# Sliding-window attention and a gated convolution block in one kernel: queries of each head in four runs of 144, one copy of x, nine buffers for layer one

## Chip, cores and metric

One core of a Trainium2 chip runs the whole problem in one program. The metric is the device time of an execution in microseconds, the median of three runs.

## The reference

```python
def _attn_ref(q, k, v):                      # 8 batches, 8 heads, 576 positions, 64 wide
    scores = scale * np.matmul(q, k.transpose(0, 1, 3, 2))
    rel = pos[:, None] - pos[None, :]
    mask_plain = (rel >= 0) & (rel < 32)                         # heads 0 to 3
    mask_dil = (rel >= 0) & (rel < 128) & (rel % 4 == 0)         # heads 4 to 7
    attn = softmax(np.where(mask, scores, -1e9))
    return np.matmul(attn, v)

def _moe_ref(x, w_in, conv_w, w_out):        # x: 576 x 512, w_in: 512 x 1024, w_out: 1024 x 512
    h = np.maximum(x @ w_in, 0.0)
    conv_out = conv_w[0] * h[t-1] + conv_w[1] * h[t] + conv_w[2] * h[t+1]
    gate = 1.0 / (1.0 + np.exp(-conv_out))
    return h * gate @ w_out
```

The attention of the eight heads, laid side by side, is x. All inputs are float32, except that the weights reach the kernel as float64.

## The kernel before, in words

The work of a batch is four attention units and one expert. A unit (`attention(b, p)`) is a pair of heads: p = 0, 1 are plain pairs (kind 0), p = 2, 3 dilated ones (kind 1). Each head's 576 queries are cut into 18 blocks of 32; a block sees 64 keys. For kind 1 the positions are first sorted by their remainder modulo 4, which makes four runs of 144 positions, and the two heads of a pair lie on partitions 0 to 63 and 64 to 127 of the tile `qk`.

A unit runs in these steps. **Scores** (L258): one float32 matmul for each block and head, 64 rows by 32 columns of the array, 64 moving columns; each is carried out as two passes. The 32 blocks 0 to 15 of the two heads go round eight places of the array (two row halves by four column quadrants). Blocks 16 and 17 go to slot 8, each head to two quadrants of its own; for kind 1 each of them is two accumulating matmuls, because it joins two runs. So kind 0 has 36 matmuls (72 passes) and kind 1 has 40 (80 passes). **Softmax**: VectorE adds the mask while it takes the scores out of PSUM (L270), then maximum, exponential, sum, reciprocal, product and a 32x32 transpose into `pt`; in the eight units of batches 0 and 1 ("slotwise") the exponential is nine small ScalarE instructions (L279). **Values** (L306): 48 float32 matmuls (96 passes), 32 rows by 64 columns. In both kinds head 0 of turn t reads row quadrant t and head 1 row quadrant t+2, so that eight matmuls in a row use eight places. The sixteen queries at the end of each run are the tail: for kind 0, eight matmuls of 32 columns, for kind 1 sixteen of 16 columns, and both go round four places only. **x**: ScalarE copies the result out of PSUM in two pieces (512 and 64 columns, L344) as the rounded part x a; the rest x b is made on VectorE in two pieces (L361), or, in the eight units of batches 0 and 1 ("helped"), by TensorE subtracting x a (L351, L354) and ScalarE copying twice (L359).

The expert of a batch: **layer one** (L386) is 192 matmuls of 128x128 by 288 columns into PSUM buffers `mm` (`mm` and `nn` for batch 0), which ScalarE takes out as `h` (L393, three buffers of `h`); the **gating** of each of eight `h` is a scaled copy and a sigmoid on ScalarE (L404, L409), two convolution taps, a product and a subtraction on VectorE (L398, L411, L415) and a copy on ScalarE (L413); **layer two** (L431) is 96 or 120 matmuls of 512 columns (batch 0: 192 of 256 columns), copied out (L441) and stored. Eight chunks of weights are converted from float64 by VectorE and ScalarE (L495 to L510), four for each layer.

Scores, values and the helped subtraction share one PSUM buffer, `att` (four banks), so only one unit at a time can be between its scores and their mask, or between its values and x. `qk` has two buffers, `v`, `s` three, `pt` two, `x` seven.

The order is not written by hand. Every step is a `Task` with an engine, a cost and a due time from the table `DUE`; `Planner.order` runs through them once while the kernel is built: of the tasks that could start within 0.25 of the earliest one, the smallest due time goes first. All engines and the SyncE queue then run their instructions in this fixed order.

Of the kernel before, what the change touches and what calls it, by code (L numbers as in the profile page):

```python
# [34 lines left out]
F32 = mybir.dt.float32  # L35
F32R = mybir.dt.float32r
BF16 = mybir.dt.bfloat16
# [10 lines left out]
W = 64  # L48
# [3 lines left out]
RES, RL = 4, S // 4  # L52
QD = 512 + 96
GW = S + 64
PAIRED = 1024
KP, KD = S + 32, S + 4 * 32 + 16
# [3 lines left out]
    "first": (72.60, 66.90, 228.40, 589.20, 119.60, 531.50, -87.70, 234.00),  # L60
    "gated": (82.90, 155.90, 204.60, -64.70, 127.90, -15.10, -48.50, 110.30),
    "second": (-142.00, 377.30, 377.60, 656.90, 397.40, 693.20, 129.60, 375.60),
    "weights": (22.30, 130.00, 960.40, -10.60, 117.40, 161.20, -241.40, 43.40),
    "fetch": (-112.90, -48.10, -47.30, -45.60, -28.50, 201.40, 419.40, 547.40),
    "conv": -231.90,
    "scores": ((-40.40, 79.70, 181.60, 63.80), (575.40, -0.50, -254.50, -6.60), (-12.70, 246.70, 160.70, 78.10), (268.20, 239.00, 217.70, 56.80), (487.10, 188.70, 220.00, 145.40), (395.00, 150.90, 159.50, -40.20), (543.40, 173.10, 228.00, 68.60), (-21.90, 798.30, 440.60, 187.40)),
    "softmax": ((12.30, -11.50, -273.80, 13.00), (22.20, -301.50, 79.30, 22.70), (-286.10, -37.40, 501.50, 612.80), (635.70, 444.80, 605.40, -27.20), (153.60, 396.90, 188.40, 295.10), (656.80, 106.40, -81.80, -42.50), (235.70, -1.40, -85.60, 184.20), (232.80, 6.50, 691.70, 114.60)),
    "values": ((-76.40, -82.10, -0.30, 335.00), (-211.50, 25.20, 1.90, -28.10), (116.70, -15.80, -40.30, -53.90), (-11.40, 77.90, 236.90, -27.60), (-87.20, -68.40, 562.90, 200.90), (59.40, -256.40, 258.50, -9.80), (-14.50, -9.70, 112.40, 606.40), (45.10, -17.50, 111.30, 181.20)),
    "queries": ((-58.30, -253.50, -98.80, -122.30), (-54.90, -11.80, -3.80, -15.00), (110.30, 156.80, 72.10, 148.70), (8.70, 82.80, 166.20, 190.90), (186.60, 202.10, 242.60, 251.80), (233.50, 430.00, 377.50, 300.80), (394.10, 432.30, 301.90, 701.90), (873.40, 615.20, 466.90, 684.00)),
    "runs": ((19.00, 45.50, -38.60, -73.00), (115.60, 104.90, 122.90, -52.00), (115.50, 92.60, 155.60, 124.30), (164.20, 194.60, 225.50, 235.00), (285.30, 234.30, 338.60, 404.50), (368.80, 827.50, 555.70, 555.10), (848.60, 650.80, 306.50, 543.70), (874.70, 433.60, 855.90, 838.60)),  # L70
# [102 lines left out]
def attn_moe(ctx: ExitStack, tc: tile.TileContext, qk_p, qk_d, v_p, v_d, w_in, w_out, conv, mask, out):  # L173
# [19 lines left out]
    slots("qk", 2, [128, QD + KD])  # L193
# [7 lines left out]
    hs = slots("h", 3, [128, S + 2])  # L201
# [22 lines left out]
    def queries(p, qk, hd, n):  # L224

        qk = qk[hd * 64:hd * 64 + 64]
        if p < 2:
            return [(qk[:, n * 32:n * 32 + 32], qk[:, S + n * 32:S + n * 32 + W])]
        key = lambda r, i: qk[:, QD + r * (RL + 32) + i * 32:QD + r * (RL + 32) + i * 32 + W]
        if n < 16:  # L230
            return [(qk[:, n * 32:n * 32 + 32], key(n // 4, n % 4))]
        g = n - 16
        q0 = 512 + g * 48
        return [(qk[:, q0 + 16 * i:q0 + 16 * i + 32], key(2 * g + i, 4)) for i in range(2)]
# [3 lines left out]
    def attention(b, p):  # L238
# [5 lines left out]
        n = (S + KP, QD + KD)[kind]  # L244
# [3 lines left out]
            out=v.t, in_=(v_p, v_d)[kind][b, p % 2]), uses=[v])  # L248

        def scores():  # L250


            for n in [4 * t + i for i in range(4) for t in range(4)] + [16, 17]:
                for hd in range(2):
                    slot, quad = place(hd, n)
                    parts = queries(p, qk.t, hd, n)
                    for i, (q, k) in enumerate(parts):
                        nc.tensor.matmul(sc.t[quad * 32:quad * 32 + 32, slot // 4, slot % 4 * W:slot % 4 * W + W], q, k,  # L258
                                         start=i == 0, stop=i == len(parts) - 1, skip_group_check=True)

        last = plan.add("PE", (0.8, 0.92)[kind], due, scores, [lq], [qk, sc, s], "S")
# [12 lines left out]
        if slotwise:  # L274
# [7 lines left out]
            last = plan.add("ACT", 2.7, soft + 1.5, exps, [last], [s, m, z], "exp")  # L282
# [15 lines left out]
        def values():  # L298
# [18 lines left out]
            for kh in range(2):  # L317
                for r in range(1 + kind):
                    for g, hd in turns[:4]:
                        c0 = 512 + 32 * kh  # L320
                        if kind == 0:
                            pv(2 * hd + g, hd, g, 10 + kh, c0, 128, 32)
                        else:
                            pv(2 * hd + g, hd, g, 8 + 2 * kh + r, c0 + 16 * r, 128 + 16 * r, 16)

        last = plan.add("PE", (0.9, 0.85)[kind], val + 0.0, values, [lv, last], [v, pt, tv, x], "V")

        def parts(t):

            main, rest = t[:, 0:512], t[:, 512:S]  # L330
            if kind == 0:
                return main.rearrange("c (q m) -> c q m", q=4), rest.rearrange("c (g m) -> c g m", g=2)
            return main.rearrange("c (m r) -> c m r", r=RES), rest.rearrange("c (m g r) -> c m g r", g=2, r=2)

        def src(i):
            main, rest = tv.t[:, :, 0:128], tv.t[:, 0:2, 128:160]
            if kind == 0:
                return (main, rest)[i]
            return (main.rearrange("c r m -> c m r"), rest.rearrange("c g (r m) -> c m g r", r=2))[i]

        pieces = (0, 0.62), (1, 0.25)
        his = []
        for i, cost in pieces[::-1]:
            last = plan.add("ACT", cost, val + 1.0, lambda i=i: nc.scalar.copy(out=parts(x.t[0])[i], in_=src(i)),  # L344
                            [last, *his], [tv, x])
            his.append(last)
# [275 lines left out]
```

## Time and profile before

| | |
|---|---|
| median of 3 runs | 536.16 us (535.06 to 536.45) |
| the profiled execution | 535.56 us, its span 533.8 us |
| TensorE matmul busy | 505.9 us, 95% of the span |
| VectorE busy | 397.3 us, 74% |
| ScalarE busy | 303.7 us, 57% |
| bytes moved | 52.24 MB, 98 GB/s on average |

The span runs from the first to the last instruction; the time lies 1.8 us above it. Matmul time is counted from an instruction's start to its end, and since matmuls are pipelined, starts and their distances tell more than busy time.

### The profile page before, as it was taken

How to read it: one execution, taken by the hardware profiler on the slowest of the kernel's cores; microseconds unless marked ns; L12 is line 12 of the kernel's file. 1: busy time of each engine (PE TensorE's matmuls, PEld its weight loads, DVE VectorE, ACT ScalarE, POOL GpSimd, SP SyncE). 2: the span in 40 equal slices, each digit the busy share in tenths (PEclk: the TensorE clock that was granted, in tenths of full speed). 3: DMA queues.
4: the chain of work that ended last, by engine and by line, in shares of the span. 5: the costliest groups of instructions: out<-in, count | busy, mean ns of one | idle time of the engine just before them, and what ended most of it. 6: DMA issues, size and time to landing. Idle time of an engine off the chain costs nothing.

```text
span 533.8 us, 17819 instructions
## 1 busy us (share of the span) xinstructions
PE 505.9 (95%) x8048; PEld 449.4 (84%) x8048; DVE 397.3 (74%) x611; ACT 303.7 (57%) x660; POOL 1.0 (0%) x15
## 2 busy tenths in 40 slices
PE   3569999999999999999999999999999999999996
PEld 2459899998877998789977899789988899789985
DVE  5987999998986799859996569828997277607900
ACT  4975998638632587237742377517764386427710
POOL 0000000000000000000000000000000000000000
PEclk9999999999999999999999999999999999999999
DMA  8846721233145312451224401321313100110011
GB/s 301 297 164 210 241 60 31 80 127 101 43 170 163 97 32 79 154 182 59 83 67 149 148 33 48 121 96 53 104 47 119 52 2 1 59 42 1 0 50 50
DMA packets 16556, 52.24 MB, mean 98 GB/s; under 512 B 2016, under 2 KB 3168, under 8 KB 15456
## 3 DMA queue, kind: packets, MB, share of 16 engines
q1 hardware_dynamic: 16336, 51.02, 28.6%
q8 instruction: 63, 1.03, 0.8%
q14 instruction: 13, 0.11, 0.1%
q10 hardware_dynamic: 144, 0.08, 0.1%
HBM read 41.66 MB, written 9.44 MB: 96 GB/s over the span
## 4 chain that ended last, share of the span: by engine, by line
PE 80%; DVE 8%; ACT 7%; DMA 3%; issue 1%; ACTq 0%
PE nn L431 34%; PE mm L386 31%; PE att L306 8%; PE att L258 4%; ACT s L279 3%; PE nn L386 2%; DVE c L398 2%; PE att L351 1%; DMA qk<-in_qk_p_dram 1%; DVE t L501 1%; DVE wo L510 1%; ACT c L409 1%; DMA c<-in_mask_dram 1%; DVE c L411 1%; DVE g L415 1%
## 5 line engine op out<-in xcount | busy, mean ns | idle before, releaser
L431 PE MATMUL nn<-wo,g 128*128 128x512 f32 (+1 forms) x960 | 212.0, 375 | 0.0
L431 PEld LDWEIGHTS nn<-wo,g 128*128 128x128 f32 x960 | 163.4, 188 | 33.4
L398 DVE SCALAR_TENSOR_TENSOR c<-h,conv_sb,c 128x576 f32<-128x576 f32 x128 | 103.5, 816 | 32.8 <-ACT c L404 31.1
L393 ACT ACTIVATE h<-mm 128x288 f32<-128x288 f32 x120 | 48.5, 408 | 43.9 <-PE mm L386 40.8
L441 ACT COPY out<-nn 128x512 f32<-128x512 f32 (+1 forms) x40 | 21.7, 542 | 72.5 <-PE nn L431 45.1
L413 ACT CAST g<-c 128x576 fp32r<-128x576 f32 x64 | 42.4, 672 | 17.7 <-DVE c L411 15.7
L411 DVE TENSOR_TENSOR c<-c,h 128x576 f32<-128x576 f32 x64 | 47.9, 756 | 5.9 <-ACT c L409 5.4
L306 PEld LDWEIGHTS att<-pt,v 32*64 32x64 f32 x3072 | 41.2, 140 | 13.1 <-issue 8.5
L415 DVE TENSOR_TENSOR g<-c,g 128x576 fp32r<-128x576 f32 x64 | 47.6, 755 | 4.5 <-ACT g L413 3.4
L404 ACT ACTIVATE c<-h,conv_sb 128x576 f32<-128x576 f32 x64 | 49.4, 778 | 1.3
L386 PE MATMUL mm<-x1a,wi 128*128 128x288 f32 x176 | 49.7, 297 | 0.0
L258 PE MATMUL att<-qk 64*32 64x64 f32 x2432 | 36.6, 237 | 13.4 <-DMA qk<-in_qk_p_dram 5.3
L258 PEld LDWEIGHTS att<-qk 64*32 64x32 f32 x2432 | 30.4, 112 | 22.2 <-issue 7.7
L409 ACT ACTIVATE c<-c 128x576 f32<-128x576 f32 x64 | 43.2, 684 | 10.3 <-DVE c L398 9.4
L306 PE MATMUL att<-pt,v 32*64 32x64 f32 (+2 forms) x3072 | 44.7, 234 | 3.8 <-DVE s L270 1.3
L386 PE MATMUL mm<-x2a,wi 128*128 128x288 f32 x144 | 41.6, 304 | 1.3 <-ACT h L393 1.3
L386 PE MATMUL mm<-x0a,wi 128*128 128x288 f32 x144 | 40.6, 297 | 0.0
L270 DVE TENSOR_TENSOR s<-att,mask_sb 128x512 f32<-128x512 f32 x64 | 26.6, 450 | 16.3 <-PE att L258 16.2
L386 PE MATMUL mm<-x6a,wi 128*128 128x288 f32 x128 | 36.6, 301 | 0.8 <-ACT h L393 0.7
L386 PE MATMUL mm<-x5a,wi 128*128 128x288 f32 x128 | 36.2, 298 | 0.2 <-ACT h L393 0.2
L386 PE MATMUL mm<-x4a,wi 128*128 128x288 f32 x128 | 35.9, 295 | 0.0
L295 DVE STREAM_TRANSPOSE pt<-s 128x576 f32<-128x576 f32 x32 | 24.8, 776 | 11.9 <-PE att L306 10.9
(134 smaller groups left out, 808.7 us busy)
## 6 DMA issues: line engine op xcount, KB each, us to landing
qk<-in_qk_d_dram SPq DMA_DIRECT2D x16, 664.0 KB, 4.3
qk<-in_qk_p_dram SPq DMA_DIRECT2D x16, 592.0 KB, 4.1
out_dram<-out SPq DMA_DIRECT2D x28, 256.0 KB, 2.2
v<-in_v_d_dram SPq DMA_DIRECT2D x16, 384.0 KB, 3.1
v<-in_v_p_dram SPq DMA_DIRECT2D x16, 384.0 KB, 3.4
raw<-in_w_in_dram SPq DMA_DIRECT2D x4, 1024.0 KB, 6.6
raw<-in_w_out_dram SPq DMA_DIRECT2D x4, 1024.0 KB, 4.7
out_dram<-out SPq DMA_DIRECT2D x16, 128.0 KB, 2.4
```

The costliest lines, as they stand in the source:

```text
L258: nc.tensor.matmul(sc.t[quad * 32:quad * 32 + 32, slot // 4, slot % 4 * W:slot % 4 * W + W], q, k, start=i == 0, stop=i == len(parts) - 1, ...
L270: last = plan.add("DVE", cost, soft + 0.0, lambda i=i: nc.vector.tensor_tensor(out=two(flat())[i], in0=scored()[i], in1=two(masked)[i], op ...
L306: nc.tensor.matmul(tv.t[hd * 64:hd * 64 + 64, bank, o:o + n], v.t[quad * 32:quad * 32 + 32, block // 2, block % 2 * 64:block % 2 * 64 + 64 ...
L386: nc.tensor.matmul(ps.t[:, 0:HALF], wi[jw][fc // 2][:, fc % 2, k], x[k].t[jx][:, hf * HALF:hf * HALF + HALF], start=(k == 0 and i == 0), s ...
L393: relu.append(plan.add("ACT", 0.4, due + 1.6 * u + 1.6, lambda fc=fc, hf=hf, ps=ps: nc.scalar.activation(out=h[fc].t[:, 1 + hf * HALF:1 + ...
L398: nc.vector.scalar_tensor_tensor(out=c[fc].t, in0=h[fc].t[:, k:S + k], scalar=conv_sb[:, k, fc:fc + 1], in1=c[fc].t, op0=ALU.mult, op1=ALU ...
L404: t = plan.add("ACT", 0.777, d, lambda fc=fc: nc.scalar.activation(out=c[fc].t, in_=h[fc].t[:, 1:S + 1], func=AF.Copy, scale=conv_sb[:, 1, ...
L409: t = plan.add("ACT", 0.686, d + 1.0, lambda fc=fc: nc.scalar.activation(out=c[fc].t, in_=c[fc].t, func=AF.Sigmoid), [t], [c[fc]], "sigmoid")
L411: t = plan.add("DVE", 0.755, d + 1.5, lambda fc=fc: nc.vector.tensor_tensor(out=c[fc].t, in0=c[fc].t, in1=h[fc].t[:, 1:S + 1], op=ALU.mult ...
L413: hi = plan.add("ACT", 0.675, d + 2.0, lambda fc=fc: nc.scalar.copy(out=half(fc, 0), in_=c[fc].t), [t, *(done[fc] if odd else [])], [c[fc] ...
L415: lo = plan.add("DVE", 0.755, d + 2.5, lambda fc=fc: nc.vector.tensor_tensor(out=half(fc, 1), in0=c[fc].t, in1=half(fc, 0).bitcast(F32), o ...
L431: nc.tensor.matmul(ps.t[:, 0:n], g[k // 2].t[:, k % 2, jg, c0:c0 + 128], w.rearrange("p h c -> p (h c)") if hf is None else w[:, hf], star ...
```

## The change

In both kinds a head's queries are now four runs of 144; run t goes to quadrant t, for both heads. The last 16 queries of run t of both heads share the 32 rows of quadrant t in slot 8: the queries are laid out with zeros under the other head, and one score matmul over all 128 rows makes both heads' scores. These four matmuls come first. Scores thus have 36 matmuls in both kinds. In values both heads of turn t read row quadrant t; the tail has sixteen matmuls of 16 columns in both kinds, going round eight places; two matmuls of kind 0 over padding alone are left out. x is copied in one piece of 576 columns, and the helped subtraction is four matmuls of 144 columns in place of four of 128 and two of 32. `h` has nine buffers. The `DUE` table is replaced whole, so the order of nearly all work moves; some planner costs change. The `qk` transfers grow from 592 and 664 KB to 632 and 680 KB, those of `v` of kind 1 shrink from 384 to 320 KB. One argument of the program's builder makes room for the added buffers.

```diff
-QD = 512 + 96
+RUN = S // 4
+QW = 512 + 128
+STEP = RUN, RUN + 32
+KEYS = S + 48, S + 4 * 32 + 16
...
-    "gated": (82.90, 155.90, 204.60, -64.70, 127.90, -15.10, -48.50, 110.30),
+    "gated": (72.60, 108.70, 165.20, -533.50, -421.40, -309.30, -197.20, -85.10),
...
+    "first": (46.20, 95.20, 158.50, 268.60, 380.70, 492.80, 604.90, 717.00),
+    "second": (90.90, 130.50, 184.50, 314.50, 426.60, 538.70, 650.80, 762.90),
+    "weights": (38.20, 30.60, 52.90, 23.00, 72.20, 63.70, 97.50, 103.60),
...
-    "scores": ((-40.40, 79.70, 181.60, 63.80), (575.40, -0.50, -254.50, -6.60), ...
+    "scores": ((6.50, 3.90, 14.10, 11.10), (30.60, 38.60, 44.30, 54.30), (141.40, 129.00, 132.30, 71.80), (190.00, 196.50, 181.20, 159.10), ...
-    "softmax": ((12.30, -11.50, -273.80, 13.00), (22.20, -301.50, 79.30, 22.70), (-286.10, -37.40, 501.50, 612.80), ...
+    "softmax": ((8.10, 6.20, 17.80, 13.70), (35.90, 39.90, 52.90, 55.90), (144.50, 138.30, 135.70, 147.30), (476.20, 505.30, 467.40, 496.50), ...
-    "values": ((-76.40, -82.10, -0.30, 335.00), (-211.50, 25.20, 1.90, -28.10), ...
+    "values": ((24.70, 17.50, 28.00, 34.00), (63.40, 49.00, 60.70, 68.70), (156.30, 149.80, 143.70, 153.10), (11.80, 65.80, -191.00, -13.70), ...
...
-    hs = slots("h", 3, [128, S + 2])
+    hs = slots("h", 9, [128, S + 2])
...
-            return 4 * hd + n % 4, (n // 4 + 2 * hd) % 4
-        return 8, 2 * hd + n - 16
+            return 4 * hd + n % 4, n // 4
+        return 8, n - 16
+
+    def query(kind, qk, hd, n):
+
+        t, i = (n // 4, n % 4) if n < 16 else (n - 16, 4)
+        k0 = QW + STEP[kind] * t + 32 * i
+        rows = slice(hd * 64, hd * 64 + 64) if n < 16 else slice(0, 128)
+        return qk[rows, n * 32:n * 32 + 32], qk[rows, k0:k0 + W]
...
+            main = [(4 * t + i, hd) for i in range(4) for t in range(4) for hd in range(2)]
+            for n, hd in [(16 + t, 0) for t in range(4)] + main:
+                slot, quad = place(hd, n)
+                nc.tensor.matmul(sc.t[quad * 32:quad * 32 + 32, slot // 4, slot % 4 * W:slot % 4 * W + W],
+                                 *query(kind, qk.t, hd, n), start=True, stop=True,
+                                 skip_group_check=True)
...
-                    pv((t + 2 * hd) % 4, hd, t, 2 * (i - kind) + hd, hd * 256 + max(64 * i - 32, 0), lo, hi - lo)
+                for t, hd in turns[2 if i == 0 else 0:]:
+                    pv(t, hd, t, i - kind, hd * 256 + max(64 * i - 32, 0), lo, hi - lo)
+            for i in (4, 5):
+                for t, hd in turns:
+                    pv(t, hd, t, i - kind, 512 + 32 * (i - 4) + 16 * hd, 128, 16)
...
+        last = plan.add("ACT", 0.68, val + 1.0, lambda: nc.scalar.copy(out=made(x.t[0])[0], in_=made(x.t[0])[1]), [last], [tv, x])
...
+                    nc.tensor.matmul(tv.t[:, t, 0:RUN], minus, part(x.t[0])[:, t], start=False, stop=True,
+                                     skip_group_check=True)
...
+            nc.vector.tensor_tensor(out=out, in0=whole, in1=made(x.t[0].bitcast(F32))[0], op=ALU.subtract)
```

From batch 3 on, each row of the new `DUE` is the row before it plus 112.1.

## Rows read from the trace of the kernel before

**Rows 1.** Busy time by engine in four stretches of the span.
```profile
0.00:60.00 60.00, 38.39 (x1188) 34.61 (x1189) 47.18 (x80) 42.29 (x189) 1.01 (x15) 1.00 0.69 245
60.00:140.00 80.00, 78.41 (x986) 75.16 (x985) 75.34 (x101) 60.37 (x113) 0.00 (x0) 1.00 0.27 89
140.00:520.00 380.00, 379.34 (x5836) 332.15 (x5836) 274.76 (x432) 199.92 (x358) 0.00 (x0) 1.00 0.24 78
520.00:533.80 13.80, 9.74 (x42) 7.48 (x40) 0.00 (x0) 1.17 (x2) 0.00 (x0) 0.98 0.15 58
```

**Rows 2.** Chain that ended last, in order of time: start, length, what.
```profile
0.74 4.52 DMA c<-in_mask_dram
...
9.37 3.10 ACT s L279 x18
...
502.44 27.32 PE nn L431 x117
```

**Rows 3.** Timeline of TensorE, scores of kind 0 between the two layers.
```profile
328.98 0.29 PE L386 MATMUL mm<-x4b,wi 128*128 128x288 f32 x1
329.11 0.29 PE L386 MATMUL mm<-x4a,wi 128*128 128x288 f32 x1
329.34 0.97 PE L258 MATMUL att<-qk 64*32 64x64 f32 x72
330.24 0.50 PE L431 MATMUL nn<-wo,g 128*128 128x512 f32 x1
```

**Rows 4.** Timeline of TensorE, scores of kind 1.
```profile
276.67 1.13 PE L258 MATMUL att<-qk 64*32 64x64 f32 x80
277.73 0.50 PE L431 MATMUL nn<-wo,g 128*128 128x512 f32 x1
```

**Rows 5.** Timeline of TensorE, values of kind 0 (first form 32x32).
```profile
346.31 1.26 PE L306 MATMUL att<-pt,v 32*64 32x32 f32 x96
347.50 0.73 PE L431 MATMUL nn<-wo,g 128*128 128x512 f32 x2
```

**Rows 6.** Timeline of TensorE, values of kind 1 (first form 32x64).
```profile
282.69 1.36 PE L306 MATMUL att<-pt,v 32*64 32x64 f32 x96
283.98 0.73 PE L431 MATMUL nn<-wo,g 128*128 128x512 f32 x2
```

**Rows 7.** Timeline of TensorE, layer one right after values.
```profile
82.08 0.40 PE L386 MATMUL nn<-x1a,wi 128*128 128x288 f32 x1
82.32 0.29 PE L386 MATMUL nn<-x1b,wi 128*128 128x288 f32 x1
82.45 0.29 PE L386 MATMUL nn<-x1a,wi 128*128 128x288 f32 x1
```

**Rows 8.** Timeline of TensorE in the front.
```profile
16.03 1.34 PE L258 MATMUL att<-qk 64*32 64x64 f32 x72 [1.02 <-DVE s L270]
19.25 0.94 PE L258 MATMUL att<-qk 64*32 64x64 f32 x45 [1.88 <-DVE s L270]
...
22.51 2.05 PE L306 MATMUL att<-pt,v 32*64 32x64 f32 x96 [1.26 <-DVE s L270]
...
28.06 2.06 PE L306 MATMUL att<-pt,v 32*64 32x64 f32 x96 [0.79 <-ACT x0b L359]
...
39.02 1.86 PE L306 MATMUL att<-pt,v 32*64 32x32 f32 x96 [0.84 <-issue]
```

**Rows 9.** Timeline of VectorE in the front.
```profile
14.49 0.78 DVE L295 STREAM_TRANSPOSE pt<-s 128x576 f32<-128x576 f32 x1
...
18.42 0.78 DVE L270 TENSOR_TENSOR s<-att,mask_sb 128x512 f32<-128x512 f32 x2
```

**Rows 10.** Groups by line and form: busy us, mean ns.
```profile
L398 DVE SCALAR_TENSOR_TENSOR c<-h,conv_sb,c 128x576 f32<-128x576 f32 x128 | 103.5, 816 | 32.8 <-ACT c L404 31.1
L411 DVE TENSOR_TENSOR c<-c,h 128x576 f32<-128x576 f32 x64 | 47.9, 756 | 5.9 <-ACT c L409 5.4
L415 DVE TENSOR_TENSOR g<-c,g 128x576 fp32r<-128x576 f32 x64 | 47.6, 755 | 4.5 <-ACT g L413 3.4
...
L344 ACT CAST x1a<-att 128x512 fp32r<-128x512 f32 x6 | 3.6, 593 | 0.0
...
L344 ACT CAST x1a<-att 128x64 fp32r<-128x64 f32 x6 | 1.3, 213 | 14.4 <-PE att L306 14.4
```

**Rows 11.** Timeline of TensorE, one helped subtraction inside layer one.
```profile
62.32 0.56 PE L351 MATMUL att<-x4a,minus 128*128 128x128 f32 x4
62.71 0.34 PE L354 MATMUL att<-x4a,minus 128*128 128x32 f32 x2
62.90 0.39 PE L386 MATMUL nn<-x0a,wi 128*128 128x288 f32 x1
```

More of the change, by code (lines that the diff above doesn't have):

```diff
@@ L247, in attention @@
         lv = plan.add("SP", 1.35, RUNS[b][p], lambda: nc.sync.dma_start(
-            out=v.t, in_=(v_p, v_d)[kind][b, p % 2]), uses=[v])
+            out=v.t[:, 0:NV - kind], in_=(v_p, v_d)[kind][b, p % 2]), uses=[v])
         def scores():
[L253 to L261, printed above, removed]
+            main = [(4 * t + i, hd) for i in range(4) for t in range(4) for hd in range(2)]
[4 more added lines that the diff above has]
+                                 skip_group_check=True)
+        last = plan.add("PE", 0.85, due, scores, [lq], [qk, sc, s], "S")
         flat = lambda: s.t[:, :, 0:W]
@@ L341, in attention, with part @@
[L341 to L346, printed above, removed]
+                    pv(t, hd, t, i - kind, 512 + 32 * (i - 4) + 16 * hd, 128, 16)
+        last = plan.add("PE", (1.1, 0.95)[kind], val + 0.0, values, [lv, last], [v, pt, tv, x], "V")
+        def part(t):
+            return t.rearrange("c (t m) -> c t m", t=4) if kind == 0 else t.rearrange("c (m t) -> c t m", t=4)
@@ L353, in less @@
-                for g in range(2):
-                    nc.tensor.matmul(tv.t[:, g, 128:160], minus,
-                                     rest[:, g] if kind == 0 else rest[:, :, g].rearrange("c m r -> c r m"), start=False,
-                                     stop=True, skip_group_check=True)
-            last = plan.add("PE", 0.6, val + 1.2, less, his, [tv, x], "E")
-            return [plan.add("ACT", cost, val + 1.5, lambda i=i: nc.scalar.copy(out=parts(x.t[1])[i], in_=src(i)),
-                             [last], [tv, x]) for i, cost in pieces]
@@ L361, in attention @@
[L361 to L363 removed]
+                    nc.tensor.matmul(tv.t[:, t, 0:RUN], minus, part(x.t[0])[:, t], start=False, stop=True,
+                                     skip_group_check=True)
+            last = plan.add("PE", 0.5, val + 1.2, less, [last], [tv, x], "E")
@@ L366, in attn_moe, with low @@
+            return [plan.add("ACT", 0.68, val + 1.5, lambda: nc.scalar.copy(
+                out=made(x.t[1])[0], in_=made(x.t[1])[1]), [last], [tv, x])]
+        def low():
+            out, whole = made(x.t[1])
+            nc.vector.tensor_tensor(out=out, in0=whole, in1=made(x.t[0].bitcast(F32))[0], op=ALU.subtract)
+        return [plan.add("DVE", 0.77, val + 1.5, low, [last], [tv, x])]
     TERMS = ((0, 0), (0, 1), (1, 0))
@@ L589, in _layouts @@
     quad, real = np.arange(128)[:, None] // 32, ok & (j >= 32)
-    first = [np.where(quad == q, real, ok) for q in (0, 2)]
+    first = np.where(quad == 0, real, ok)
     qq = ql % 16
@@ L593, in _layouts @@
     import ml_dtypes
-    mask = np.where(np.stack([*first, ok, real, left], 1), np.float32(0), neg).astype(ml_dtypes.bfloat16)
+    mask = np.where(np.stack([first, ok, real, left], 1), np.float32(0), neg).astype(ml_dtypes.bfloat16)
     return {
```

125 lines of the change are left out of this document (45 added, 80 removed).

## The prediction

> **What bounds the kernel now.** I read the table by stretches first [rows 1]. TensorE has 38.4 us of work in the first 60, 78.4 of the next 80, and 379.3 of 380 after that: from 60 to 520 us it is without a matmul for only 1.59 + 0.66 = 2.3 us. VectorE has 47.2 of the first 60, 75.3 of the next 80, and then 275 of 380. So there are two stages. In the front, up to about 60 us, TensorE is short of work (60 - 38.4 = 21.6 us idle); VectorE is the fullest engine there, but not full. Behind that TensorE is the bound and VectorE has a quarter to spare. The chain of waits [rows 2] says the same: it starts with a transfer of 4.5 us, goes through exponentials of 3.10 us a unit on ScalarE, and ends with 117 matmuls of layer two back to back in 27.32 us. The end is thus as late as the sum of TensorE's work plus what TensorE lacked in front, and three things can move it: the length of TensorE's attention work, the front, and new holes behind the front.
>
> Prices on TensorE are taken from start to start. Scores of kind 0, 72 passes, hold it from 329.34 to 330.24, 0.90 us [rows 3]; of kind 1, 80 passes, for 1.06 [rows 4]. Values of kind 0 hold it 1.19 [rows 5], of kind 1 1.29 [rows 6], with 96 passes each.
>
> **Values.** Kind 0 has 80 passes on eight places and a tail of 16 on four; kind 1 has 64 and 32. If a pass costs a on eight places and b on four, 16 (b - a) = 1.29 - 1.19 = 0.10, so b is a + 6.25 ns. There is also a fixed part for the change of the array's layout: layer one to scores starts 0.23 apart where two matmuls of layer one are 0.13 apart [rows 3], so 0.10. Then 96 a + 0.10 + 0.10 = 1.19: a is 10.3 ns, b 16.6. After the change everything runs on eight places: kind 0 has 54 matmuls, 108 a + 0.10 = 1.21 (+0.02), kind 1 96 a + 0.10 = 1.09 (-0.20). Over 16 units of each: **-2.9 us**. The trace has no 16-column passes on eight places. If these cost half of b, 8.3 ns, kind 0 is 76 a + 0.27 + 0.10 = 1.15 and kind 1 64 a + 0.37 = 1.03: -4.8 us. If they cost b, kind 0 gains 12 b, +0.20, and kind 1 nothing: +3.2 us. I take the middle, since the 80 passes of kind 0 on eight places are the nearest rows.
>
> The order within the eight places changes too: head 0 and head 1 of a turn now follow one another on the same row quadrant, where before the quadrants alternated. Scores already use four column places on each row half, at 12.5 and 13.3 ns a pass (0.90 / 72, 1.06 / 80) [rows 3, 4], so column places that share rows do overlap, and I cost this order at nothing; the first rival is its price. The Trainium skill (TensorE: Matmul & The Clock Gate, "The mechanism" and what overlaps there) speaks against me: a weight load overlaps running matmuls only if it goes to other rows. No row here has two neighbouring matmuls of different columns on the same rows, so this trace does not settle it. By the rule as it stands the time would be that rival's.
>
> **Scores.** The 8 extra passes of kind 1 cost 1.06 - 0.90 = 0.16, 20 ns each, all on four places. Now every unit has 64 passes on eight places (0.90 - 8 x 0.020 = 0.74 with the fixed part) and 8 on four column quadrants over all rows: at 20 ns that is 0.90 again, plus a change of layout between the two, at 0.10 like that of layer one to scores: 1.00. Kind 0 loses 0.10, kind 1 gains 0.06: **+0.6 us** in 32 units. With no price for the change of layout and passes at a: 0.74 + 0.08 = 0.82, -5.1 us. With a full price, in (0.10) and out again (after values the first layer-one matmul is 0.24 ahead of the next where 0.13 is the rule, 0.11 [rows 7]): 1.11, +4.2 us. I take the middle. The Trainium skill (TensorEngine Tiling (Array Packing), "Key Properties") says that a change of tiling mode, not just of the tile, drains the engine. By it a price is due, as at the change that rows 3 show (0.10); without one the sum would be lower by 0.10 x 32 = 3.2 us.
>
> **Helped subtraction.** Four matmuls take 62.71 - 62.32 = 0.39 and two take 0.19 [rows 11]. Four of 144 columns come to 0.39 x 144 / 128 = 0.44: -0.14 in each of eight units, -1.1 us where TensorE is the bound, nothing where it waits anyway. Half the units are in the front: **-0.6 us**.
>
> **One copy of x.** Two ScalarE copies of 0.593 and 0.213 [rows 10] become one; on 576 columns it takes at most their sum, 0.81. ScalarE and VectorE have room behind the front, so I put nothing down; in the front the two overlap and the gain is under 0.1 a copy. The larger and smaller transfers change by under 64 KB; in the front they delay or speed a landing by tenths of a us, which the front's range covers.
>
> **Nine buffers of h, and the new order.** Behind the front TensorE lacks 2.3 us in all [rows 1], so more buffers there can give at most that; I put down nothing. Both matter in the front. Before, the first unit's transpose is done at 14.49 + 0.78 = 15.3 [rows 9], yet its values start at 22.51, waiting for a mask addition, because `att` first serves the fourth scores (16.03) and fifth scores (19.25) [rows 8]. In the new table the values of batch 0 (17.5 to 34) come after the scores of batch 0 (3.9 to 14.1) but ahead of batch 1 (30.6 and more). So the first values can start when the fourth scores are taken out, 18.42 + 0.78 = 19.2 [rows 9]: 3.3 us earlier. The units then follow one another at 28.06 - 22.51 = 5.5 us [rows 8], bound by `att` and its copies, so the gain is handed on to layer one. What stands in its way: the fourth unit's exponentials, 3.10 us on ScalarE [rows 2], can hold up the first copy of x. I take **-2.5 us**. Bounds: nothing, if VectorE, with weights to convert too, gives the time back; and -7.5, all that VectorE has idle in the first 60 us (12.8) behind the mask's landing at 5.3 [rows 1, 2]. The end of the run moves with it, as the last 117 matmuls have no gap to swallow it.
>
> **Sum**: -2.9 + 0.6 - 0.6 - 2.5 = -5.4 us against the profiled execution's 535.56, 530.2. The median of the runs lies 0.6 above that execution, so I forecast **530.8 us**.
>
> **Rivals.**
> *Same rows, one after the other.* If two neighbours on the same rows can't overlap, eight places work as four: all passes of values cost b. Kind 0 is 108 b + 0.10 = 1.89 (+0.70), kind 1 96 b + 0.10 = 1.69 (+0.40): +17.6 us, and with the other terms (-2.5) the time is about 551. It decides from +0.17 us a unit on. For it: the order is new, and four places are slower than eight here. Against it: scores overlap on shared rows.
> *Softmax starves.* From batch 3 on the table puts gating (-533 and up) far ahead of softmax (467 and up) for every batch, so on VectorE a softmax step only goes when no gating step can start. Gating takes 8 x (2 x 0.816 + 0.756 + 0.755) = 25.1 us of VectorE a batch [rows 10], about as long as layer one lasts (192 x 0.13 = 25). If one unit a batch comes too late, layer one of the next batch waits for its x: at the 5.5 us that a unit takes in the front, five batches cost 27 us, 558 us in all. It outweighs the gain from 1.1 us a batch on. Against it: VectorE has 28% idle from 140 to 520 [rows 1], and x has seven buffers.
> *The front gains all it can.* -7.5 in place of -2.5 and values at their low end: 524 us. Nine buffers let layer one of batch 1 run while batch 0 is still to be gated, which speaks for it; VectorE at 75.3 of 80 us right behind the front [rows 1] speaks against.
> *Nothing comes of it.* Scores at their full price (+4.2) and the tail of values at b (+3.2) against the front and the subtraction (-3.1): +4.3, 540; with only one of the two, about 535 to 536.
>
> **Chances.** The forecast and its neighbourhood, 527 to 534: 0.45. The front's full gain, 519 to 527: 0.17. Nothing, 534 to 541: 0.16. Same rows: 0.10. Starved softmax: 0.12. A measurement of this kernel can tell 0.3%, 1.6 us, from no change: faster means below 534.5, slower above 537.8. Faster is 0.45 + 0.17 = 0.62 less a little at the border, with the upper end of "nothing" among the slower: 0.61, 0.11 for the same, 0.28 slower. The range that leaves out no more than two in ten reaches over the whole gain of the front and into the rivals that cost: 519 to 546; the likeliest case alone has 527 to 534.
>
> **What will show it.** Values: 1.21 and 1.09 us from start to start of the next layer; near 1.7 to 1.9 means the first rival. Scores: 1.00 in both kinds; 0.82 or 1.11 are the ends. First values at 19 to 21 us and TensorE idle for 18 to 20 us in the first 60. Behind 140 us TensorE idle for under 2 us; layer one waiting for x or ScalarE waiting for values there means the second rival. The prediction fails above all if the front, which I know only by one path through it, moves by more than 5 us, or if holes open behind it.

## The result, and the profile after

The change makes the kernel faster: 530.52 us, the median of 5 runs (529.23 to 531.16), against 535.28 of the kernel before in 5 runs (534.09 to 536.45); the ratio is 0.9908 with a 95% interval of 0.9885 to 0.9931, that is 4.9 us less. The forecast was 530.8. The profiled execution takes 530.94 us, its span is 529.1.

The stretches of the kernel after, with the columns of [rows 1]:

```profile
0.00:60.00 60.00, 40.09 (x1147) 35.86 (x1148) 47.86 (x81) 42.22 (x154) 1.41 (x27) 0.97 0.66 235
60.00:140.00 80.00, 78.98 (x1110) 74.56 (x1109) 77.23 (x105) 59.84 (x131) 0.00 (x0) 1.00 0.27 97
140.00:520.00 380.00, 378.50 (x5830) 329.91 (x5821) 268.92 (x404) 206.26 (x339) 0.00 (x0) 1.00 0.25 78
```

TensorE is without a matmul for 1.02 + 1.50 = 2.5 us from 60 to 520 us, before for 2.3 [rows 1]. So nothing was gained there, and no hole opened either. Its busy time in the first 60 us grew by 1.7 us.

TensorE's timeline in front:

```profile
18.70 1.24 PE L302 MATMUL att<-pt,v 32*64 32x32 f32 x61 [1.72 <-DVE s L266]
...
25.83 1.87 PE L302 MATMUL att<-pt,v 32*64 32x32 f32 x108 [2.40 <-ACT x0b L337]
...
30.30 1.67 PE L302 MATMUL att<-pt,v 32*64 32x64 f32 x92 [0.73 <-ACT x1b L337]
...
32.50 0.61 PE L367 MATMUL mm<-x1a,wi 128*128 128x288 f32 x1
...
33.14 0.44 PE L367 MATMUL mm<-x1a,wi 128*128 128x288 f32 x1
33.38 0.44 PE L367 MATMUL mm<-x0a,wi 128*128 128x288 f32 x1
...
37.75 0.29 PE L367 MATMUL mm<-x2b,wi 128*128 128x288 f32 x1
37.88 0.29 PE L367 MATMUL mm<-x2a,wi 128*128 128x288 f32 x1
...
38.89 1.21 PE L302 MATMUL att<-pt,v 32*64 32x64 f32 x96
```

The first values start at 18.70, where they started at 22.51, and the second at 25.83 instead of 28.06 [rows 8]. The fourth start at 38.89 in place of 39.02: the head start of the units is used up, but layer one (L367) now begins at 32.50, between the third and fourth values, and no longer after the fourth (40.81). The chain of waits shows what eats the first 1.6 us of the head start of 3.8, and where the gain ends up:

```profile
22.25 3.01 ACT s L275 x18
25.26 0.53 ACT x0b L337
...
497.98 27.31 PE nn L412 x117
```

The second copy of x waits on ScalarE behind 3.01 us of exponentials, as the prediction feared. The last 117 matmuls of layer two start at 497.98 instead of 502.44 [rows 2], 4.46 us earlier, and take as long as before. The rest of the span's difference of 4.7 us lies behind them.

How much work of the two layers is done early can be counted: matmuls of layer one in the first two stretches and of layer two in the second. First the kernel before (L386, L431):

```profile
0.00:60.00 60.00, 13.20 (x76) 11.64 (x77) 1.00 0.69 245
60.00:140.00 80.00, 44.01 (x310) 41.28 (x308) 1.00 0.27 89
60.00:140.00 80.00, 27.66 (x212) 26.09 (x213) 1.00 0.27 89
```

Then the kernel after (L367, L412):

```profile
0.00:60.00 60.00, 19.24 (x108) 17.45 (x108) 0.97 0.66 235
60.00:140.00 80.00, 39.96 (x276) 37.18 (x276) 1.00 0.27 97
60.00:140.00 80.00, 32.76 (x231) 29.91 (x231) 1.00 0.27 97
```

By 60 us there are 108 matmuls of layer one in place of 76. By 140 us layer one is level (384 in both by their starts; a matmul that lies across the end of a stretch is counted twice above) and layer two is 19 ahead, all of them matmuls of 512 columns, since the 192 of batch 0 are done in both. At 27.31 / 117 = 0.233 us each that is 4.4 us, nearly the whole gain. The scores of an eleventh unit are done as well, before those of ten.

What the attention costs TensorE is read in the steady part: values of kind 0, then values, scores and values of kind 1, each followed by layer two:

```profile
278.07 1.33 PE L302 MATMUL att<-pt,v 32*64 32x32 f32 x108
279.33 4.94 PE L412 MATMUL nn<-wo,g 128*128 128x512 f32 x20
...
326.87 1.21 PE L302 MATMUL att<-pt,v 32*64 32x64 f32 x96
328.01 2.37 PE L412 MATMUL nn<-wo,g 128*128 128x512 f32 x9
330.31 1.11 PE L253 MATMUL att<-qk 128*32 128x64 f32 x72
331.35 1.66 PE L412 MATMUL nn<-wo,g 128*128 128x512 f32 x6
```

From start to start, values take 1.26 us in kind 0 and 1.14 in kind 1, before 1.19 and 1.29 [rows 5, 6]; scores take 1.04 in either kind, before 0.90 and 1.06 [rows 3, 4]. Over 16 units of each kind that is +1.1 - 2.4 + 2.2 - 0.3 = +0.6 us: TensorE's attention work behind the front did not get shorter. So the gain must have come from the front.

### The profile page after: what moved, and what is told of

It is laid out like the page before. It is cut to its first block, busy times and chain, and to the rows that moved or that the text cites. A ratio compares the mean times of both kernels' runs of the same rounds, so it can differ in the third digit from the quotient of the medians.

```text
span 529.1 us, 17823 instructions
## 1 busy us (share of the span) xinstructions
PE 502.9 (95%) x8096; PEld 444.2 (84%) x8096; DVE 394.0 (74%) x588; ACT 309.2 (58%) x624; POOL 1.4 (0%) x27
## 4 chain that ended last, share of the span: by engine, by line
PE 92%; ACT 3%; DVE 2%; DMA 2%; issue 1%; SPq 0%; ACTq 0%; DVEq 0%
PE nn L412 39%; PE mm L367 37%; PE att L302 8%; PE att L253 6%; PE nn L367 2%; ACT s L275 1%; DMA qk<-in_qk_p_dram 1%; DMA v<-in_v_p_dram 1%; DVE s L266 1%; PE att L333 1%; DVE pt L291 0%; DVE s L289 0%; DVE m L268 0%; ACT L390 0%; ACT c L390 0%
## 5 line engine op out<-in xcount | busy, mean ns | idle before, releaser
L412 PE MATMUL nn<-wo,g 128*128 128x512 f32 (+1 forms) x960 | 213.1, 375 | 0.0
L412 PEld LDWEIGHTS nn<-wo,g 128*128 128x128 f32 x960 | 163.6, 188 | 33.2 <-ACT out L422 0.4
L379 DVE SCALAR_TENSOR_TENSOR c<-h,conv_sb,c 128x576 f32<-128x576 f32 x128 | 103.2, 815 | 16.5 <-ACT c L385 15.3
L374 ACT ACTIVATE h<-mm 128x288 f32<-128x288 f32 x120 | 48.7, 407 | 43.7 <-PE mm L367 43.4
L302 PEld LDWEIGHTS att<-pt,v 32*64 32x64 f32 x3264 | 39.8, 137 | 17.9 <-issue 10.7
L392 DVE TENSOR_TENSOR c<-c,h 128x576 f32<-128x576 f32 x64 | 47.9, 757 | 4.5 <-ACT c L390 2.9
L302 PE MATMUL att<-pt,v 32*64 32x64 f32 (+2 forms) x3264 | 43.5, 230 | 7.3 <-ACT x0b L337 2.4
L253 PE MATMUL att<-qk 64*32 64x64 f32 (+1 forms) x2304 | 37.3, 235 | 13.5 <-DMA qk<-in_qk_p_dram 5.3
L253 PEld LDWEIGHTS att<-qk 64*32 64x32 f32 (+1 forms) x2304 | 28.4, 111 | 24.0 <-DMA qk<-in_qk_p_dram 5.3
L367 PE MATMUL mm<-x6a,wi 128*128 128x288 f32 x160 | 45.0, 296 | 0.0
L367 PE MATMUL mm<-x1a,wi 128*128 128x288 f32 x144 | 41.8, 305 | 0.0
L367 PE MATMUL mm<-x0a,wi 128*128 128x288 f32 x144 | 41.5, 303 | 0.0
L367 PE MATMUL mm<-x3a,wi 128*128 128x288 f32 x144 | 41.0, 300 | 0.0
L367 PE MATMUL mm<-x5a,wi 128*128 128x288 f32 x128 | 36.1, 297 | 0.2 <-ACT h L374 0.2
L367 PE MATMUL mm<-x4a,wi 128*128 128x288 f32 x128 | 36.1, 297 | 0.0
L367 PE MATMUL mm<-x2a,wi 128*128 128x288 f32 x112 | 32.0, 301 | 0.0
```

Of the source, the lines that this page charges most:

```text
L367: nc.tensor.matmul(ps.t[:, 0:HALF], wi[jw][fc // 2][:, fc % 2, k], x[k].t[jx][:, hf * HALF:hf * HALF + HALF], start=(k == 0 and i == 0), s ...
L374: relu.append(plan.add("ACT", 0.4, due + 1.6 * u + 1.6, lambda fc=fc, hf=hf, ps=ps: nc.scalar.activation(out=h[fc].t[:, 1 + hf * HALF:1 + ...
L379: nc.vector.scalar_tensor_tensor(out=c[fc].t, in0=h[fc].t[:, k:S + k], scalar=conv_sb[:, k, fc:fc + 1], in1=c[fc].t, op0=ALU.mult, op1=ALU ...
L392: t = plan.add("DVE", 0.755, d + 1.5, lambda fc=fc: nc.vector.tensor_tensor(out=c[fc].t, in0=c[fc].t, in1=h[fc].t[:, 1:S + 1], op=ALU.mult ...
L412: nc.tensor.matmul(ps.t[:, 0:n], g[k // 2].t[:, k % 2, jg, c0:c0 + 128], w.rearrange("p h c -> p (h c)") if hf is None else w[:, hf], star ...
```

## The experiments

The theory was that the gain is made of the two halves that the prediction named: less attention work through the layout, and an earlier start of layer one through the order. The rivals were that one half did it all, and that the nine buffers of `h`, which the prediction put down at nothing, are what lets the order work.

**The two halves apart.** The first kernel has the attention layout of before, its transfers and its two-piece copies, in exactly the order of the kernel after and with nine `h`:

```diff
-                    pv(t, hd, t, i - kind, hd * 256 + max(64 * i - 32, 0), lo, hi - lo)
+                    pv((t + 2 * hd) % 4, hd, t, 2 * (i - kind) + hd, hd * 256 + max(64 * i - 32, 0), lo, hi - lo)
...
-        last = plan.add("ACT", 0.68, val + 1.0, lambda: nc.scalar.copy(out=made(x.t[0])[0], in_=made(x.t[0])[1]), [last], [tv, x])
+        last = plan.add("ACT", 0.68, val + 1.0, lambda: both(copy(0), (1, 0)), [last], [tv, x])
```

> The attention of the kernel before (places, tail, two-piece copies, the transfers) under exactly the order of the changed kernel, with its nine buffers of h. If the gain is the order's (theory: layout about -0.5 us by the measured prices of scores +0.14 and -0.02, values +0.07 and -0.15, subtraction -0.14 in eight units), this is about 531 us, ratio 0.992. If the recorded terms hold (order -2.5, layout -2.9), 532.8, ratio 0.9955. If order and layout only work together, nothing: 0.998 to 1.002.

Measured: 531.40 us (529.24 to 533.41, 6 runs), ratio 0.992, interval 0.9888 to 0.9951. In its trace, the values of kind 1 and the scores have the prices of before:

```profile
326.96 1.36 PE L306 MATMUL att<-pt,v 32*64 32x64 f32 x96
328.25 2.37 PE L429 MATMUL nn<-wo,g 128*128 128x512 f32 x9
330.55 0.97 PE L258 MATMUL att<-qk 64*32 64x64 f32 x72
331.45 1.66 PE L429 MATMUL nn<-wo,g 128*128 128x512 f32 x6
```

1.29 and 0.90, and yet the time is that of the kernel after within the intervals. It has done 109 matmuls of layer one by 60 us, and from 60 to 140 us 231 of layer two, just like the kernel after: the lead does not need the layout.

The second kernel is the opposite: the new layout and the single copy, in exactly the order of before and with three `h`:

```diff
-    "first": (46.20, 95.20, 158.50, 268.60, 380.70, 492.80, 604.90, 717.00),
+    "first": (72.60, 66.90, 228.40, 589.20, 119.60, 531.50, -87.70, 234.00),
...
-    hs = slots("h", 9, [128, S + 2])
+    hs = slots("h", 3, [128, S + 2])
```

> The attention of the changed kernel under exactly the order of the kernel before, with three buffers of h. Theory by the measured prices: -0.5 us, ratio 0.999. By the recorded terms: -2.9 us, ratio 0.9946. If order and layout only work together: slower than before, 1.002 or more.

Measured: 534.25 us (532.98 to 536.00, 12 runs), ratio 0.9981, interval 0.9964 to 0.9998: 1.0 us faster. The ratios of the halves, -4.3 and -1.0 us, add up to -5.3, the whole has -4.9. So by the medians the order with its nine `h` carries some four fifths of the gain, the layout about one fifth; the intervals are wide (2.6 to 6.0 and 0.1 to 1.9 us).

Since the second kernel issues its work in exactly the order of before, the two traces can be laid side by side. In the kernel before the second values start at 28.06 [rows 8]. The third of before, then the second and third of this kernel:

```profile
33.16 1.87 PE L306 MATMUL att<-pt,v 32*64 32x32 f32 x96 [0.79 <-ACT x1b L359]
```

```profile
28.07 1.69 PE L302 MATMUL att<-pt,v 32*64 32x64 f32 x96 [0.73 <-ACT x0b L342]
...
32.35 1.87 PE L302 MATMUL att<-pt,v 32*64 32x32 f32 x108 [0.73 <-ACT x1b L342]
```

A unit of kind 1 holds `att` for 4.28 us in place of 5.10, by shorter values, subtraction and copies. Layer one starts 1.25 us earlier (39.56), by 140 us ten matmuls of layer two more are done (222), and the last 117 start at 500.84, 1.6 us earlier. From 140 to 500 us the kernel loses 0.7 us against before, about what the steady prices say. So the layout's gain arises in the front as well, where units wait for one another through `att`, and not in the length of TensorE's work.

**The buffers of h.** The kernel after with three, its order planned anew from the same table; then with six:

```diff
-    hs = slots("h", 9, [128, S + 2])
+    hs = slots("h", 3, [128, S + 2])
```

> The changed kernel with three buffers of h in place of nine; the same table of due times, so the planner puts layer one and gating in another order by itself. If the nine buffers are what lets layer one of batch 1 run ahead in the front, 3 to 5 us of the gain go: ratio 0.997 to 1.0. If the early start of values and layer one makes the gain, under 1 us goes: 0.991 to 0.993.

> The changed kernel with six buffers of h. With three, TensorE stood still from about 70 to 83 us, since the weights come before gating there and layer one had no free h. If each buffer carries layer one on by 3.2 us of that, six leave about 9 of the 27 us: ratio 1.005 to 1.01. If it needs all eight of a batch, it stays near 1.03; if six are enough, 0.991.

Measured: with three 557.36 us (556.31 to 561.13, 6 runs), ratio 1.0414 (1.0382 to 1.0446); with six 554.72 us (553.01 to 557.89, 6 runs), ratio 1.0355 (1.0324 to 1.0386). Against the kernel after, three buffers lose 27 us, far more than either theory had. The stretches with three `h` show where, with the columns of [rows 1]:

```profile
60.00:70.00 10.00, 6.25 (x241) 5.41 (x233) 9.76 (x15) 7.42 (x30) 0.00 (x0) 0.94 0.59 210
70.00:80.00 10.00, 0.00 (x0) 0.00 (x0) 9.76 (x13) 5.48 (x18) 0.00 (x0) 0.50 0.56 186
80.00:90.00 10.00, 6.49 (x29) 6.49 (x30) 9.25 (x13) 7.61 (x15) 0.00 (x0) 0.53 0.21 90
```

TensorE has no matmul at all from 70 to 80 us, while VectorE is full. The longest wait of its matmuls between 60 and 140 us (total, times, longest), ScalarE's timeline and VectorE's name the links of it:

```profile
PE nn L367 <- ACT h L374: 14.2, 2, 14.0
```

```profile
83.05 0.71 ACT L374 ACTIVATE h<-nn 128x288 f32<-128x288 f32 x2 [0.25 <-DVE c L392]
```

```profile
77.03 1.22 DVE L491 SCALAR_TENSOR_TENSOR wo<-raw 128x1024 fp32r<-128x1024 uint32 x1
78.18 3.98 DVE L379 SCALAR_TENSOR_TENSOR c<-h,conv_sb,c 128x576 f32<-128x576 f32 x5
```

Layer one waits for ScalarE to take out its buffer into an `h` (L374), and ScalarE for a step of gating on VectorE that reads an `h` (L392). No `h` is free, because gating (L379) comes only after the conversion of weights (L491) on VectorE, at 78.18. In the kernel after the order on VectorE is much the same:

```profile
76.28 1.23 DVE L491 SCALAR_TENSOR_TENSOR wo<-raw 128x1024 fp32r<-128x1024 uint32 x1
77.42 3.25 DVE L379 SCALAR_TENSOR_TENSOR c<-h,conv_sb,c 128x576 f32<-128x576 f32 x4
```

Its gating starts no earlier, at 77.42 (before: 64.00). But there the eight `h` of batch 0 can wait, and one more, so layer one goes on. Six buffers hold too few of the eight: in that kernel TensorE has 15.52, 12.32 and 16.56 us of work in the three 20 us stretches from 60 to 120, the kernel after 18.99, 19.99 and 20.00. The granted clock there is 0.94, 0.67 and 0.71 with six, 1.00 in the kernel after, so even the work that is done takes longer. The buffers are thus not an extra: under this table nine, which hold a whole batch, carry the order, and six do not. Seven and eight were not run, nor nine buffers with the table of before, so what the buffers are worth without the new order is not known.

**The fifth scores.** The prediction drew the gain of the front from one thing: that the fifth unit's scores no longer stand in `att` ahead of the first values. This kernel puts them back, with their transfer:

```diff
-    "scores": ((6.50, 3.90, 14.10, 11.10), (30.60, 38.60, 44.30, 54.30), ...
+    "scores": ((6.50, 3.90, 14.10, 11.10), (16.00, 38.60, 44.30, 54.30), ...
-    "queries": ((2.20, 0.10, 8.80, 7.40), (22.90, 32.60, 39.80, 46.30), ...
+    "queries": ((2.20, 0.10, 8.80, 7.40), (11.00, 32.60, 39.80, 46.30), ...
```

> The changed kernel with the fifth scores (batch 1) due at 16.0 in place of 30.6 and their transfer at 11.0 in place of 22.9, so that they go through att before the first values, as in the kernel before. By the recorded step (the first values start earlier because the fifth scores no longer stand ahead) 2 to 3 us of the gain go: ratio 0.995 to 0.997. If the gain is in the order of weights and gating, under 1 us goes: 0.990 to 0.993.

Measured: 541.79 us (540.36 to 543.83, 6 runs), ratio 1.0107 (1.0088 to 1.0125). That is 11 us more than the kernel after and 6 more than before, where 2 to 3 were expected. TensorE's timeline, then VectorE's, in that kernel:

```profile
19.61 1.95 PE L253 MATMUL att<-qk 128*32 128x64 f32 x72 [1.66 <-DVE s L266]
27.47 1.87 PE L302 MATMUL att<-pt,v 32*64 32x32 f32 x108 [5.91 <-issue]
```

```profile
24.49 1.23 DVE L491 SCALAR_TENSOR_TENSOR wi<-raw 128x1024 fp32r<-128x1024 uint32 x1
...
26.55 0.81 DVE L266 TENSOR_TENSOR s<-att,mask_sb 128x512 f32<-128x512 f32 x2
```

The fifth scores end at 21.56 and stay in `att` until VectorE takes them out, from 26.55 to 27.36. Ahead of that it converts weights. The first values start 0.11 us behind that, at 27.47, though the profile names no semaphore for their wait (their releaser reads "issue"). By 60 us only 61 matmuls of layer one are done. So the path that the prediction named exists, and its price is set by what VectorE has in hand when the buffer is full. The edit moved the planned order of everything behind it too, and the granted clock is 0.50 from 52.0 to 58.8 us, so the 11 us are not this wait alone.

**Neighbours on the same rows.** Two kernels for the first rival. In one the quadrants of the two heads alternate again, all else being as after; in the other each place does all of its matmuls before the next place begins:

```diff
-            turns = [(t, hd) for t in range(4) for hd in range(2)]
+            turns = [((t + 2 * hd) % 4, hd) for t in range(4) for hd in range(2)]
-                for t, hd in turns[2 if i == 0 else 0:]:
+                for t, hd in [x for x in turns if i or x[0]]:
```

```diff
-            for i in range(kind, 5):
-                lo, hi = max(32 * i - 32, 0), min(32 * i + 32, 128)
-                for t, hd in turns[2 if i == 0 else 0:]:
...
+            for t, hd in turns:
+                for i in range(kind, 5):
+                    if i or t:
```

> The changed kernel with values issued so that neighbours alternate row quadrants (0, 2, 1, 3, 2, 0, 3, 1) as before, on the same eight places and the same data. If neighbours on the same rows cost nothing, values stay at 1.26 and 1.14 us from start to start and the ratio at 0.991. If a load waits for its neighbour on the same rows, they fall by 0.1 or more, and with 32 units the ratio to 0.985 or less.

> The changed kernel with all values matmuls of one place issued one after the other, then the next place. If the number of places in turn sets the pace of a pass, values grow well past 1.26 and 1.14 us: at the 58 ns between two passes on one place that four places at about 14.6 ns give, 108 and 96 passes come to 5.6 to 6.3 us. If the pace is set by the issue of passes alone, they stay near 1.2.

Measured: alternating, 529.26 us (528.45 to 530.25, 4 runs), ratio 0.989 (0.9856 to 0.9925), the time of the kernel after. Its values of kind 0 and kind 1:

```profile
279.05 1.33 PE L302 MATMUL att<-pt,v 32*64 32x32 f32 x108
280.31 3.99 PE L412 MATMUL nn<-wo,g 128*128 128x512 f32 x16
...
327.82 1.21 PE L302 MATMUL att<-pt,v 32*64 32x64 f32 x96
328.96 2.37 PE L412 MATMUL nn<-wo,g 128*128 128x512 f32 x9
```

1.26 and 1.14, to the hundredth as with neighbours on the same rows. The Trainium skill (TensorE: Matmul & The Clock Gate, "The mechanism") says that a weight load overlaps running matmuls only on other rows; as a price of this order no run here shows it. Place by place, a single run gives 705.64 us. Its values of kind 1 and of kind 0, both at a granted clock of 1.00:

```profile
281.12 4.32 PE L302 MATMUL att<-pt,v 32*64 32x64 f32 x96
285.37 3.90 PE L412 MATMUL nn<-wo,g 128*128 128x512 f32 x9
...
304.23 5.02 PE L302 MATMUL att<-pt,v 32*64 32x64 f32 x108
309.18 6.00 PE L412 MATMUL nn<-wo,g 128*128 128x512 f32 x18
```

4.25 / 96 = 44 ns and 4.95 / 108 = 46 ns a pass, where 58 was worked out ahead from four places (5.6 to 6.3 us a unit). So with eight places in turn it makes no difference which of them share rows, and with one place after another the pace falls to a quarter. A place here also writes to a PSUM bank and half of its own, so neighbours in one place share their target too; the runs do not tell the two apart.

**The tail of scores.** In one kernel the four tail matmuls keep to 64 rows, so that the array's tile shape stays one (the second head's scores of its last 16 queries are left out); in the other the tail comes last:

```diff
-        rows = slice(hd * 64, hd * 64 + 64) if n < 16 else slice(0, 128)
+        rows = slice(hd * 64, hd * 64 + 64)
```

```diff
-            for n, hd in [(16 + t, 0) for t in range(4)] + main:
+            for n, hd in main + [(16 + t, 0) for t in range(4)]:
```

> The four tail matmuls of scores use rows 0 to 63 only, so that all scores matmuls have one tile shape; the scores of the second head's last 16 queries of each run are left out. If the change of layout inside scores costs 0.10 to 0.14, scores take 0.90 to 0.94 us in place of 1.04. If it costs nothing and the tail's four places do, they stay at 1.02 to 1.04.

> The four tail matmuls of scores over all 128 rows come last in place of first. If a change of layout costs the same wherever it stands, scores stay at 1.04 us and the ratio at 0.991. If the change from 128 rows by 32 columns to the layers' 128 by 128 is cheaper than that from 64 by 32, the two together cost less: 0.95 us, and 32 units give 2 to 3 us: ratio 0.986.

Measured: 528.68 us in a single run, and 529.98 us (529.74 to 531.34, 4 runs), ratio 0.9914 (0.9883 to 0.9945). Scores with the tail on 64 rows:

```profile
330.16 0.97 PE L253 MATMUL att<-qk 64*32 64x64 f32 x72
331.06 1.67 PE L412 MATMUL nn<-wo,g 128*128 128x512 f32 x6
```

0.90 us in place of 1.04 for the same 72 passes: the change of tile shape inside a unit costs 0.14 us. The trace of the kernel after shows the spot: in all 21 units of scores between 140 and 500 us the first matmul on 64 rows starts 0.149 us behind the last on 128, where neighbours of one shape start at most 0.06 apart. With the tail last it is 1.04 again, so it is the change that costs, not its place. By this 32 units would give back 4.5 us, but the single run is only 1.8 us below the median of the kernel after. Side by side (the order is the same), the profiled executions agree with the price: the kernel with the tail on 64 rows gains 2.8 us from 140 to 500 us, 0.14 in 21 units being 2.9. But it reaches 139 us 0.7 us later than the kernel after, so the shorter scores bring nothing in the front.

**Versions that might do better.** The exponentials that held up x were cut into three tasks of the planner, between which a copy can go. Then the layouts were mixed, by the prices: kind 0 as before (0.90 and 1.19), kind 1 as after (1.04 and 1.14), in the order of the kernel after. Last, both together:

```diff
-            def exps():
-                for i in range(9):
+            def exps(j):
+                for i in range(3 * j, 3 * j + 3):
...
-            last = plan.add("ACT", 3.1, soft + 1.5, exps, [last], [s, m, z], "exp")
+            for j in range(3):
+                last = plan.add("ACT", 1.03, soft + 1.5, lambda j=j: exps(j), [last], [s, m, z], "exp")
```

```diff
+                    if kind:
+                        pv(t, hd, t, i - 1, c0, lo, hi - lo)
+                    else:
+                        pv((t + 2 * hd) % 4, hd, t, 2 * i + hd, c0, lo, hi - lo)
```

> The changed kernel with the nine exponentials of a slotwise unit planned as three tasks of three, so that a copy of x can go between them; nothing else. In the changed kernel the second copy of the first x waits about 1.8 us behind the 3.0 us of exponentials. If the chain through the one att buffer sets the front, 1 to 2 us are gained against the changed kernel: ratio 0.987 to 0.989. If VectorE's share sets it, nothing: 0.990 to 0.992.

> The changed kernel with kind 0 laid out as before (scores 0.90, values 1.19 us) and kind 1 as changed (1.04 and 1.14), under exactly the changed kernel's order, with nine buffers of h. If the prices of one unit add up, kind 0 saves 0.14 + 0.07 = 0.21 us in 16 units, 3.4 us less the extra copies: 527.5 us, ratio 0.985. If shorter attention only leaves TensorE idle elsewhere, 0.990 to 0.992 as for the changed kernel.

> The mixed layout, and the exponentials of a slotwise unit planned as three tasks. If the two gains add up: 1.3 us below the mixed layout, ratio 0.983. If the order of the front was at its best for tasks of nine, no different from the mixed layout.

Measured: split, 529.17 us (528.64 to 530.80, 5 runs), ratio 0.9888 (0.9859 to 0.9917); mixed, 531.42 us (529.73 to 534.08, 6 runs), ratio 0.9914 (0.9893 to 0.9935); both, 531.66 us (531.08 to 534.93, 6 runs), ratio 0.9924 (0.9902 to 0.9945). With the exponentials split, layer one starts at 31.26, 1.2 us earlier, and the median is the lowest of all that were run in several rounds; but its interval overlaps that of the kernel after, so it is not shown to be better. The mixed layout has the steady prices it was made for and gains nothing. Its layer one starts at 35.09, not 32.50. Most of that is one gap in the middle of the first unit's values, behind 61 of the 96 matmul passes:

```profile
22.62 0.88 PE L307 MATMUL att<-pt,v 32*64 32x64 f32 x35 [2.78 <-issue]
```

The kernel after has a gap at the same spot, at 20.65, of 0.71 us. The mixed kernel reaches 139 us 1.8 us later than the kernel after and gains 1.1 us from there to 500. Why the same order leaves so long a gap there isn't settled.

## Why the prediction was right in its sum and wrong in its terms

The total was forecast at -5.4 us and came out at -4.9 by the ratio. Two errors of opposite sign lie below it; that they cancel is luck. So is part of the 0.3 us by which the time itself was missed (530.8 against 530.5): the kernel before has 535.28 in the five runs of the comparison, and the forecast started from 536.16.

**The layout was forecast at -2.9 us (values -2.9, scores +0.6, subtraction -0.6), and alone it gave -1.0, between -1.9 and -0.1.**
- *Values*, the mis-sized term: -1.3 us by the steady prices. Kind 0 has 1.26 instead of the forecast 1.21, kind 1 has 1.14 instead of 1.09. The price of a pass was right: the 12 passes more in kind 0 cost 1.26 - 1.14 = 0.12, 10 ns each. What was too small is the fixed part: 1.14 - 96 x 0.010 = 0.18, where the prediction had 0.10. It took the way into the layout [rows 3], which lies ahead of the first start and is not in these times at all; in them is the way out, 0.13 us from the last pass to layer two. With 0.18 for the fixed part, a pass on four places cost 3 to 5 ns more than one on eight (0.05 / 16 and 0.15 / 32), not 6.25, and so the gain of leaving them was smaller.
- *Scores*: +1.9 us (0.14 x 16 - 0.02 x 16) instead of +0.6. The middle between no price and a full one was too low. The change of tile shape costs 0.14, not 0.10. The Trainium skill (TensorEngine Tiling (Array Packing), "Key Properties") says that changing the tiling mode drains the engine; the trace agrees, by 0.14 us.
- *Helped subtraction*: the right direction. In the steady pace of layer one after, the four matmuls starting at 40.94 hold it until 41.45, 0.51 us, before 0.58 [rows 11]. That is a gain of 0.07, half the forecast, in a term of tenths.

**The front was forecast at -2.5 us; the order with its buffers gave -4.3.** The first step was right: the first values start at 18.70 (forecast 19.2) because no fifth scores stand in `att`, and the run with them put back loses more than the whole gain. The obstacle was right too, the exponentials that hold up x. But that path is not what the gain came through: the head start of 3.8 us is gone by the fourth values (38.89 against 39.02). What remains is that layer one starts at 32.50 with three units done, and from there to 60 us TensorE is without a matmul for only 1.9 us, around 44 us.

**The failed step is "more buffers there can give at most that; I put down nothing".** The nine `h` were weighed by the idle time of TensorE that the old order shows, 2.3 us [rows 1]. Of the front it said that both matter, without a price for the buffers. But a buffer's worth depends on the order: the new table puts gating behind the conversions, and with three `h` it has a hole of 14.0 us and takes 557 us. With nine, conversions come first, layer one runs on, and by 140 us TensorE is 4.4 us ahead. The prediction mentioned the mechanism only in a rival ("the front gains all it can").

**The rivals.** *Same rows, one after the other*: refuted, values of 1.14 and 1.26 do not depend on who is the neighbour. *Softmax starves*: not seen, TensorE is without a matmul for 1.5 us from 140 to 520. *The front gains all it can*: half right, layer one does run ahead, for 4 us and not 7.5. *Nothing comes of it*: right about attention, which costs +0.6 us in the steady part, wrong about the front.

What stays open: the layout's -1.0 us under the old order is shown to arise in the front, but each of its steps there was not timed alone, and under the new order the layout's worth (0.9908 against 0.992) is within the noise. Not known either is why the tail on 64 rows and the mixed layout lose time in the front, nor what nine buffers give under the old order.

## What to carry to other kernels

When an order is replaced together with a buffer count, cost them as one: ask how many results the new order lets stand before their consumer is due, and compare that with the buffers; here the idle time under the old order, 2.3 us, did not show it. When one part is said to save, time it alone in an order that is held fixed: here a forecast right to 0.3 us hid a layout worth a third of what was claimed. And a buffer that two steps share is held not by the step that fills it but by the one that empties it, so look at that engine's queue.

## What the runs showed of the hardware that was not expected

Small float32 matmuls take 10 ns a pass when eight places of the array take turns, whether neighbours share their rows or not, and 44 to 46 ns with one place after another.

In the kernel with values place by place the granted clock averaged 0.90 over the run, in the kernel after 1.00. From 281.0 to 285.4 us, while a unit of values ran place by place, it was 1.00; in the 3.8 us behind it, it was 0.55, most of that time at the lower level of 1.2 GHz, and nine matmuls of layer two took 3.83 us, in the kernel after 2.30. With three `h`, TensorE was busy for 6.25 of the 10 us ahead of 70 us and then stood still; the clock fell to the lower level at 68.8, was granted at 0.50 and 0.53 until 90, and rose at 89.3, with matmuls running again from 83.5. Of the 175 us that values place by place cost, the 32 units themselves explain 16 x (4.95 - 1.26) + 16 x (4.25 - 1.14) = 109; the slower layers behind them fit the rest, but that was not taken apart.

In front of the kernel after, matmuls of layer one start 0.24 us apart at 33.14 and 0.13 apart at 37.75. The stretches print a granted clock of 1.00 for both, but the trace holds no record of the clock ahead of 36.35 us, and 1.00 is printed where there is none. The pace changes about where the record begins, and 0.24 is also the pace at 48.80, in the stretch from 46.6 to 50.0 us for which the record has the lower level. In the kernel before, the record begins at 45.27; layer one goes at 0.24 up to 44.9 and at 0.13 from 46.56. So, judged by the pace, TensorE ran at the lower level up to those moments in both kernels, and the 1.00 printed for the first 60 us before [rows 1] and the 0.97 after say nothing of that time. Ahead of the fall at 46.6 TensorE had waited 1.5 us for a copy of x; whether the wait brought it about is not shown.
